# BigBird attention and a Fourier mix on one core: attention values turned into x by VectorE's 32x32 block transposes and 16 small transfers per half pair, and q and k of the last seven pairs turned by VectorE

## The chip, the cores and the metric

The kernel runs on one core of one Trainium2 chip. The time is device time of that core in microseconds (us), as the runs report it; it lies some 2 us above the span of the same run in the trace. The medians of the kernel before range from 1111.3 to 1114.8 us over the five sets of runs, some 0.3%; each experiment is therefore set against runs of the kernel before on the same chip.

## The reference

```python
def _attn_ref(q, k, v, sampled_blocks):            # B, H, S, D = 4, 8, 768, 64; float32
    scores = scale * np.matmul(q, k.transpose(0, 1, 3, 2))
    # mask: blocks of 32; neighbours, first and last block, three sampled blocks per row block
    ...
    scores = np.where(mask, scores, -1000000000.0)
    scores = scores - np.max(scores, axis=-1, keepdims=True)
    attn = np.exp(scores)
    attn = attn / (np.sum(attn, axis=-1, keepdims=True) + 1e-09)
    return np.matmul(attn, v)

def _moe_ref(x, w_ch1, w_ch2):                      # x: (4, 768, 512), the heads side by side
    mixed = np.real(np.fft.fft(np.fft.fft(x, axis=1), axis=2))
    u = x + mixed
    un = (u - mean(u)) / np.sqrt(var(u) + 1e-06)    # over the last axis
    return u + np.maximum(un @ w_ch1, 0.0) @ w_ch2  # 512 -> 2048 -> 512
```

## The kernel before

The kernel walks over 16 pairs of heads, four pairs to a batch. A pair has two halves of queries (384 each), a half has six steps over the keys, and a *slot* is two steps. Each slot issues score products, exponentials (ScalarE), for batches 1 to 3 a mask product (VectorE; in batch 0 the mask is added by a small product on TensorE), and value products into a PSUM bank `o`. Batch 0 also loads and rounds the weights in 32 chunks. From batch 1 on, the Fourier mix and the channel products of the batch before are fed in between the slots. The mixing tail of the last batch closes the run.

A half pair's values come out as head dimension by query and have to be turned into rows of `x`:

```python
def values(u):
    ...
    for i in range(2):
        nc.tensor.matmul(o[D * i:D * i + D, :], vt[:, i, c, :], e[:, i, :],
                         start=(c == 0), stop=(c == C - 1))
    if c == C - 1:
        ...
        oT = sum_p.tile([P, HS], FP32, tag="oT", name="oT")     # one buffer
        nc.scalar.copy(out=oT, in_=o_of.pop((n, half)))
        ...

def place(n, half):
    b, j = pairs[n]
    oT = o_of.pop((n, half))
    if j == 0:
        x_of[b, half] = xp.tile([P, T, DM], FP32, tag=("xA", "xB")[half], name="x")
    xt, at = ps_t.tile([P, 512], FP32, tag="t", name="xt"), bank("t")
    for c in range(T):
        nc.tensor.transpose(xt[:, c * P:(c + 1) * P], oT[:, c * P:(c + 1) * P], ident)
    nc.scalar.copy(out=x_of[b, half][:, :, j * P:(j + 1) * P],
                   in_=xt[:, 0:HS].rearrange("p (c f) -> p c f", c=T))
```

`xp` has two buffers for each half of `x`, so batch 2 writes into the memory of batch 0, whose results must have been stored from there.

The rounding of a weight chunk, in batch 0, is two instructions of ScalarE followed by five of VectorE on the chunk that a transfer of the sync queue brought:

```python
def w_load(i):
    t = room(i % ROOMS, [P, 3 * WN], "wraw", U32)
    nc.sync.dma_start(out=t[:, 0:2 * WN].bitcast(I32), in_=wchunks[i][0])
    ...
def w_round(i):
    ...
    nc.scalar.mul(out=lo.bitcast(FP32), in_=lo, mul=2.0 ** -52)
    nc.scalar.mul(out=a.bitcast(FP32), in_=hi.bitcast(FP32), mul=2.0 ** -112)
    nc.vector.tensor_scalar(out=a, in0=a, ...)             # and four more on VectorE
```

Short jobs (transposes, `place`, mask steps) wait in a list and are put between the products:

```python
while short and (s in (2, 5) or len(short) > 1 or phase == 0 or sl == B * SB):
    short.popleft()[2]()
```

Of the kernel before, what the change touches and what calls it, by code (L numbers as in the profile page):

```python
# [11 lines left out]
FP32 = mybir.dt.float32  # L12
# [6 lines left out]
ACT = mybir.ActivationFunctionType  # L19
# [45 lines left out]
           ((384, 64, 191, 64, 64, -1), (704, -128, 64, 63, 63, -1), (640, 127, 0, 1, 1, 1)))  # L65


def _rows(view, tile):

    got = []  # L70
    for t, p0, runs, jump, n, s0, step in _ORDER:
        if t != tile:
            continue
        at = view[s0:s0 + 1, :]
        row, col = list(at.ap[0])[0], list(at.ap[1])
        if jump > 0:
            got.append((p0, runs * n, bass.AP(tensor=at.tensor, offset=at.offset,
                                              ap=[[jump * row, runs], [step * row, n], col])))
            continue
        for r in range(runs):  # L80
            at = view[s0 + r * jump:s0 + r * jump + 1, :]
            got.append((p0 + r * n, n, bass.AP(tensor=at.tensor, offset=at.offset,
                                               ap=[[step * row, n], col])))
    return got
# [3 lines left out]
def kernel(  # L88
# [14 lines left out]
    nc = tc.nc  # L103

    B, H, S, D = q.shape
    DM = H * D
    FF = w_ch1.shape[1]
    P = 128
    C = S // P
    BLK = 32  # L110
    NB = S // BLK
    NR = sampled_blocks.shape[1]
    HS = S // 2
# [4 lines left out]
    T = C // 2  # L118
# [2 lines left out]
    scale = 1.0 / float(D) ** 0.5  # L121
    KA = D + NB
    NP = H // 2
    LIMIT = 400.0

    const = ctx.enter_context(tc.tile_pool(name="const", bufs=1))

    ident = const.tile([P, P], FP32, name="ident")
# [24 lines left out]
    peaks = const.tile([P, 2 * B * NP], FP32, name="peaks")  # L153

    ld = ctx.enter_context(tc.tile_pool(name="ld", bufs=1))
    ldv = ctx.enter_context(tc.tile_pool(name="ldv", bufs=2))
    tp_p = ctx.enter_context(tc.tile_pool(name="tp_p", bufs=2))
# [19 lines left out]
    def busy(engine, us, after=0.0):  # L177
        when[engine] = max(when[engine], after) + us
        return when[engine]

    def bank(tag):

        at = free[tag].index(min(free[tag]))
        when["PE"] = max(when["PE"], free[tag][at])
        free[tag][at] = float("inf")
        return tag, at

    def give(which, at):
        free[which[0]][which[1]] = at + HOP
# [3 lines left out]
    pairs = [(b, j) for b in range(B) for j in range(NP)]  # L193
    loaded, v_of = {}, {}

    def load_k(n, queue=None):

        b, j = pairs[n]
        kt = loaded.get((n, 1))
        if kt is None:  # L200
            kt = ld.tile([P, C, 2, D], FP32, tag="k", name="kr")
        for i in range(2):
            (queue or nc.sync).dma_start(out=kt[:, :, i, :],
                                         in_=k[b, 2 * j + i].rearrange("(p c) d -> p c d", p=P))
        loaded[n, 1] = kt

    def load_q(n):

        b, j = pairs[n]
        qt = loaded.get((n, 0))  # L210
        if qt is None:
            qt = loaded[n, 0] = ld.tile([P, T, 2, 2, D], FP32, tag="q", name="qr")
        for t in range(T):
            for i in range(2):
                rows = q[b, 2 * j + i][2 * P * t:2 * P * (t + 1), :]
                nc.sync.dma_start(out=qt[:, t, :, i, :],
                                  in_=rows.rearrange("(p r) d -> p r d", r=2))
# [47 lines left out]
    def warm(n):  # L265

        m = ps_m.tile([P, P], FP32, tag="m", name="warm")
        for _ in range(n):
            nc.tensor.matmul(m, ident, ident, start=True, stop=True)
# [158 lines left out]


    turned, e_of, acc_of, o_of, sums_of, x_of, sp_of = {}, {}, {}, {}, {}, {}, {}  # L430
    s_at, e_at, oT_at, acc_at = {}, {}, {}, {}

    def turn(n, a, half):

        t = loaded[n, a]
        if half == 0:
            turned[n, a] = tp_p.tile([P, S], FP32, tag="qk"[a] + "T", name="qk"[a] + "T")
        dst = turned[n, a]
        first = n == 0 and half == 0
        tag, pool = ("m", ps_m) if first and a == 0 else ("t", ps_t)  # L440
        tp, at = pool.tile([P, 512], FP32, tag=tag, name="tp"), bank(tag)
        if a == 0:
            parts = [t[:, c // 2, c % 2, :, :] for c in (range(4, 6) if half else range(4))]
        else:
            parts = [t[:, T * half + c, :, :] for c in range(T)]
        for c, part in enumerate(parts):
            nc.tensor.transpose(tp[:, c * P:(c + 1) * P], part, ident)  # L447
        done = busy("PE", 0.15 * len(parts)) + HOP
        if a == 1:
            nc.scalar.copy(out=dst[:, half * HS:(half + 1) * HS], in_=tp[:, 0:HS])  # L450
            give(at, busy("ACT", 0.5, done))
        else:
            for i, (to, to_jump, frm, jump, cnt, step) in enumerate(_TURNED[half]):
                on, copy = (("DVE", nc.vector.tensor_copy) if n == 0 and (half == 1 or i % 2 == 0)
                            else ("ACT", nc.scalar.copy))
                copy(out=_grid(dst, to, 2, to_jump, cnt, 1),
                     in_=_grid(tp, frm, 2, jump, cnt, step))
                end = busy(on, 0.27 if cnt > 1 else 0.18, done)
            give(at, end)
        if half == 1:  # L460
            flat = t.rearrange("p t r i d -> p (t r i d)" if a == 0 else "p c i d -> p (c i d)")
            nc.scalar.activation(out=flat, in_=flat, func=ACT.Square,
                                 accum_out=peaks[:, 2 * n + a:2 * n + a + 1])
            busy("ACT", 1.05)

    UP = 2 * C
    UNITS = len(pairs) * UP
# [44 lines left out]
    def values(u):  # L512
        n, w = divmod(u, UP)
        half, c = divmod(w, C)
        e = e_of[u]
        busy("PE", 0.75, e_at[u])
        vt = v_of[n]
        if c == 0:
            o_of[n, half] = ps_o.tile([P, HS], FP32, tag="o", name="o")
        o = o_of[n, half]  # L520
# [4 lines that stand above are left out]
            if half == 1:  # L525
                v_of.pop(n)
            oT = sum_p.tile([P, HS], FP32, tag="oT", name="oT")
            nc.scalar.copy(out=oT, in_=o_of.pop((n, half)))
            oT_at[n, half] = busy("ACT", 0.5, when["PE"] + HOP) + HOP
            o_of[n, half] = oT  # L530

    def place(n, half):

        b, j = pairs[n]
        oT = o_of.pop((n, half))
        if j == 0:
            x_of[b, half] = xp.tile([P, T, DM], FP32, tag=("xA", "xB")[half], name="x")
        xt, at = ps_t.tile([P, 512], FP32, tag="t", name="xt"), bank("t")
        for c in range(T):
            nc.tensor.transpose(xt[:, c * P:(c + 1) * P], oT[:, c * P:(c + 1) * P], ident)  # L540
        nc.scalar.copy(out=x_of[b, half][:, :, j * P:(j + 1) * P],
                       in_=xt[:, 0:HS].rearrange("p (c f) -> p c f", c=T))
        give(at, busy("ACT", 0.5, busy("PE", 0.45, oT_at[n, half]) + HOP))

    def into_sums(key, j, sp):
        if j == 0:
# [542 lines left out]
    COVER = 100.0  # L1089
    AHEAD = 2.2  # L1090
    ALONE = 3.0
    LEAVES = 9.0
    SP = UP // SLOT
    SB = SP * NP
    W_PACE = 1.42
# [81 lines left out]
    def slot(sl):  # L1177
# [17 lines left out]
        reuse = n % NP == 0 and phase >= 2  # L1195
        if sl > 0 and s == (5 if reuse else 3) and sl <= B * SB:
            b, j = pairs[n]
            at = oT_at[n, 0]
            if reuse:
                until(lambda: (b - 2, 0) in finished)  # L1200
                at = when["PE"] + LEAVES
            short.append(("t", at, lambda: place(n, 0)))
        if 0 < sl <= B * SB and s == 0 and n % NP != 1:
            short.append(("t", oT_at[n - 1, 1], lambda: place(n - 1, 1)))
        if sl < B * SB and n % NP == 1 and s == 1:
            b = pairs[n - 1][0]
            at = oT_at[n - 1, 1]
            if b >= 2:
                until(lambda: (b - 2, 1) in finished)
                at = when["PE"] + LEAVES  # L1210
            short.append(("t", at, lambda: place(n - 1, 1)))
        if sl > SB and s == 0 and sl <= B * SB:
            short.append(("t", acc_at[n - 1, 1], lambda: total(n - 1)))
        if n + 1 < len(pairs):
            for at, a, half in ((1, 0, 0), (2, 0, 1), (4, 1, 0), (5, 1, 1)):
                if s == at:
                    short.append(("t", 0.0, lambda a=a, half=half: turn(n + 1, a, half)))
            if s == 1:
                load_v(n + 1)
# [15 lines left out]
            channel_step()  # L1235
            gap(max(state["owed"], 0.0))

        while short and (s in (2, 5) or len(short) > 1 or phase == 0 or sl == B * SB):
            short.popleft()[2]()
        if s == 3 and n + 2 < len(pairs):  # L1240
            load_q(n + 2)
        if s == 0 and 0 < n < len(pairs) - 1:
# [26 lines left out]
    state["got"] = 2  # L1269
    turn(0, 1, 0)  # L1270
    turn(0, 0, 0)
    warm(3)
    spread_q(keep_q[0:NB, :], keep)
    w_loads()
    for sl in range(B * SB + 1):
# [112 lines left out]
```

## Time and profile before

In the lines of the profile PE is TensorE's products, PEld its loads of the fixed operand, DVE is VectorE, ACT ScalarE, POOL GpSimd, and SPq the queue of transfers that the sync engine issues. An L with a number is a line of that run's kernel.

| | before |
|---|---|
| time, median of the first 3 runs | 1117.0 us |
| span of the profiled run | 1109.3 us |
| stage 0: to the first mask product of batch 1 | 137.1 us |
| stage 1: to the first store of batch 0's results (batch 1's attention, then mixing) | 298.0 us |
| stage 2: to the first product of the last tail (batches 2 and 3) | 556.1 us |
| tail | 118.1 us |
| TensorE busy | 1067.7 us |

The prediction shows the lines of the page, the stages, the chain and the timelines. Two lines that it does not show: the share of each engine in the chain that ended last, and the granted clock of TensorE in 40 slices (9 is nine tenths of full speed or more).

```profile
PEclk9999999999999999999999999999999999999999
...
PE 85%; DVE 9%; ACT 2%; issue 2%; DMA 0%; POOL 0%; SPq 0%; ACTq 0%; DVEq 0%; POOLq 0%
```

The chain is TensorE's own work for 85% of the span, and the sync queue (SPq) and the transfers have no share of it. No slice of the clock is below 9; its mean is 0.994 (in batch 1, by the prediction's stage table, 0.97).

### The profile page before, as it was taken

How to read it: one execution, taken by the hardware profiler on the slowest of the kernel's cores; microseconds unless marked ns; L12 is line 12 of the kernel's file. 1: busy time of each engine (PE TensorE's matmuls, PEld its weight loads, DVE VectorE, ACT ScalarE, POOL GpSimd, SP SyncE). 2: the span in 40 equal slices, each digit the busy share in tenths (PEclk: the TensorE clock that was granted, in tenths of full speed). 3: DMA queues.
4: the chain of work that ended last, by engine and by line, in shares of the span. 5: the costliest groups of instructions: out<-in, count | busy, mean ns of one | idle time of the engine just before them, and what ended most of it. 6: DMA issues, size and time to landing. Idle time of an engine off the chain costs nothing.

```text
span 1109.3 us, 12468 instructions
## 1 busy us (share of the span) xinstructions
PE 1067.7 (96%) x4446; PEld 544.5 (49%) x4446; DVE 664.8 (60%) x1216; ACT 394.1 (36%) x818; POOL 274.2 (25%) x302
## 2 busy tenths in 40 slices
PE   8999988998899999999999999999999999999996
PEld 3333333544455545444444555454444555568675
DVE  5888878497754525653459355544356446575563
ACT  6788755555212102353443212244330202120210
POOL 1000088688100001245537000344540000000000
PEclk9999999999999999999999999999999999999999
DMA  7756311011000000211110000111000000100001
GB/s 219 208 176 215 93 51 43 15 45 42 1 1 1 0 1 19 66 33 27 43 29 15 1 0 1 51 50 29 1 1 0 1 1 19 39 1 1 1 16 45
DMA packets 65187, 44.30 MB, mean 40 GB/s; under 512 B 52814, under 2 KB 57948, under 8 KB 65116
## 3 DMA queue, kind: packets, MB, share of 16 engines
q1 hardware_dynamic: 63228, 42.62, 13.7%
q10 hardware_dynamic: 1856, 0.79, 0.3%
q8 instruction: 37, 0.61, 0.2%
q14 instruction: 34, 0.28, 0.1%
q0 software_dynamic: 32, 0.01, 0.0%
HBM read 37.11 MB, written 6.29 MB: 39 GB/s over the span
## 4 chain that ended last, share of the span: by engine, by line
PE 85%; DVE 9%; ACT 2%; issue 2%; DMA 0%; POOL 0%; SPq 0%; ACTq 0%; DVEq 0%; POOLq 0%
PE y L954 23%; PE z L898 15%; PE s L478 10%; PE o L522 9%; PE yp L898 7%; PE yy L1017 6%; PE xp L898 4%; DVE e L499 2%; PE tp L447 2%; PE zp L711 1%; PE sp L569 1%; PE zp L682 1%; PE xt L540 1%; PE s L483 1%; PE utp L823 1%
## 5 line engine op out<-in xcount | busy, mean ns | idle before, releaser
L509 POOL TENSOR_TENSOR acc<-acc,e 128x384 f32<-128x384 f32 x192 | 198.3, 1066 | 90.6 <-DVE e L499 90.1
L499 DVE TENSOR_TENSOR e<-s,mask 128x768 f32<-128x768 f32 x144 | 131.2, 951 | 78.4 <-ACT s L497 78.0
L478 PE MATMUL s<-qT,kT 64*128 64x384 f32 x768 | 161.7, 526 | 8.5 <-DVE e L499 7.4
L522 PE MATMUL o<-e,vr 128*64 128x384 f32 x768 | 145.1, 499 | 0.0
L497 ACT ACTIVATE s<-s 128x768 f32<-128x768 f32 x144 | 109.3, 795 | 65.5 <-PE s L478 64.9
L957 DVE TENSOR_TENSOR x<-y,x 128x512 f32<-128x512 f32 x72 | 49.8, 691 | 133.9 <-PE y L954 133.8
L954 PE MATMUL y<-w_sb,hB 128*128 128x512 f32 x288 | 128.4, 595 | 1.1 <-DVE x L957 1.0
L954 PE MATMUL y<-w_sb,hA 128*128 128x512 f32 x288 | 128.8, 594 | 0.6 <-ACT zs L713 0.6
L509 POOL TENSOR_TENSOR acc<-e 128x384 f32<-128x384 f32 x48 | 51.8, 1100 | 231.3 <-DVE e L499 173.2
L903 DVE TENSOR_TENSOR hA<-z,hA 128x384 f32<-128x384 f32 x64 | 35.7, 558 | 111.4 <-PE z L898 111.4
L478 PEld LDWEIGHTS s<-qT,kT 64*128 64x128 f32 x768 | 63.1, 187 | 68.1 <-DVE e L499 25.3
L898 PE MATMUL z<-unT,t 128*128 128x384 f32 x256 | 93.0, 486 | 0.0
L774 POOL TENSOR_SCALAR st<-st 128x1 f32<-128x1 f32 x24 | 6.6, 276 | 344.5 <-DVE st L773 344.1
L954 PEld LDWEIGHTS y<-w_sb,hB 128*128 128x128 f32 x288 | 53.3, 190 | 64.7 <-issue 62.1
L522 PEld LDWEIGHTS o<-e,vr 128*64 128x64 f32 x768 | 46.6, 136 | 73.9 <-issue 71.4
L954 PEld LDWEIGHTS y<-w_sb,hA 128*128 128x128 f32 x288 | 52.9, 190 | 59.6 <-issue 56.6
L907 ACT ACTIVATE hA<-hA 128x384 f32<-128x384 f32 x64 | 33.5, 524 | 123.6 <-DVE hA L903 123.1
L898 PEld LDWEIGHTS z<-unT,t 128*128 128x128 f32 x256 | 48.6, 190 | 33.9
L907 ACT ACTIVATE hB<-hB 128x384 f32<-128x384 f32 x64 | 33.6, 525 | 85.6 <-DVE hB L903 85.6
L898 PE MATMUL z<-t,w_sb 128*128 128x384 f32 x128 | 48.0, 499 | 3.1 <-DVE t L860 3.1
L898 PE MATMUL xp<-unT,w_sb 128*128 128x384 f32 x128 | 47.1, 491 | 1.5 <-ACT zs L713 1.1
L898 PE MATMUL yp<-unT,w_sb 128*128 128x384 f32 x128 | 46.7, 488 | 0.2 <-DVE un L747 0.2
(190 smaller groups left out, 1395.1 us busy)
## 6 DMA issues: line engine op xcount, KB each, us to landing
wraw<-in_moe_w_ch_dram SPq DMA_DIRECT2D x32, 512.0 KB
qr<-in_q_dram SPq DMA_DIRECT2D x90, 64.0 KB
vr<-in_v_dram SPq DMA_DIRECT2D x30, 192.0 KB
kr<-in_k_dram SPq DMA_DIRECT2D x28, 192.0 KB
out_dram<-x SPq DMA_DIRECT2D x16, 128.0 KB
out_dram<-x SPq DMA_DIRECT2D x8, 256.0 KB
out_dram<-x SPq DMA_DIRECT2D x8, 126.0 KB
out_dram<-x SPq DMA_DIRECT2D x4, 252.0 KB
```

The source lines that it names most:

```text
L447: nc.tensor.transpose(tp[:, c * P:(c + 1) * P], part, ident)
L478: nc.tensor.matmul(s[:, i, 0:HS], kT[D * i:D * i + D, c * P:(c + 1) * P], qT[D * i:D * i + D, half * HS:(half + 1) * HS], start=True, stop ...
L497: nc.scalar.activation(out=s[:, :, 0:HS], in_=s[:, :, 0:HS], func=ACT.Exp, scale=scale)
L499: nc.vector.tensor_tensor(out=e, in0=s[:, :, 0:HS], in1=m.broadcast_to([P, 2, HS]), op=ALU.mult)
L509: nc.gpsimd.tensor_add(out=acc, in0=e_of[u - 1][:, i, :] if c == 1 else acc, in1=e[:, i, :])
L522: nc.tensor.matmul(o[D * i:D * i + D, :], vt[:, i, c, :], e[:, i, :], start=(c == 0), stop=(c == C - 1))
L898: nc.tensor.matmul(to, a[:, k, :], c[:, k, :], start=(k == 0), stop=(k == ND // 2 - 1))
L903: tt(out=to, in0=ps, in1=a, op=ALU.add)
L907: nc.scalar.activation(out=h, in_=h, func=ACT.Relu)
L954: nc.tensor.matmul(y, hs[0, half][:, l, m * P:(m + 1) * P], w2_sb[:, 4 * r + l, :], start=(l == 0), stop=(l == 3))
L957: nc.vector.tensor_tensor(out=x[:, m, :], in0=y, in1=x[:, m, :], op=ALU.add)
L1017: nc.tensor.matmul(ps, a[:, k, :], c[k // 2][:, k % 2, :] if isinstance(c, list) else c[:, k, :], start=(k == 0), stop=(k == 3))
```

## The change

Its intent is to take transposes off TensorE, which is 96% busy. (1) The three transposes and two ScalarE copies of each of the 32 half pairs become one VectorE block transpose straight out of PSUM and 16 transfers of 32x3x32 elements (12 KB) on the sync queue, which put the turned blocks where they belong in `x`. (2) For pairs 9 to 15, q and k are loaded as blocks and turned by VectorE. (3) The choice among the short jobs, the first slots and the number of warm-up products change too.

```diff
+    BY_VECTOR = 2 * NP + 1
...
             oT = sum_p.tile([P, HS], FP32, tag="oT", name="oT")
-            nc.scalar.copy(out=oT, in_=o_of.pop((n, half)))
-            oT_at[n, half] = busy("ACT", 0.5, when["PE"] + HOP) + HOP
+            nc.vector.transpose(out=oT, in_=o_of.pop((n, half)))
+            busy("DVE", 0.5, when["PE"] + HOP)
...
     def place(n, half):
-        xt, at = ps_t.tile([P, 512], FP32, tag="t", name="xt"), bank("t")
-        for c in range(T):
-            nc.tensor.transpose(xt[:, c * P:(c + 1) * P], oT[:, c * P:(c + 1) * P], ident)
-        nc.scalar.copy(out=x_of[b, half][:, :, j * P:(j + 1) * P], ...)
+        for g in range(P // BLK):
+            for t in range(P // BLK):
+                nc.sync.dma_start(
+                    out=x_of[b, half][BLK * t:BLK * t + BLK, :, j * P + BLK * g:j * P + BLK * (g + 1)],
+                    in_=oT[BLK * g:BLK * g + BLK, :, t, :])
...
+    def flip_blocks(n, a):
+        ...
+            out = _at(kT, 0, [(1, P), (P, C)])        # k is written strided
+        nc.vector.transpose(out=out, in_=t)
...
-        while short and (s in (2, 5) or len(short) > 1 or phase == 0 or sl == B * SB):
-            short.popleft()[2]()
+        while short and (s in (2, 5) or len(short) > 1 or phase == 0 or r == 0):
+            ready = [i for i in short if max(i[1], min(free[i[0]])) <= when["PE"] + 0.1]
+            if not ready and s not in (2, 5) and r > 0:
+                break
+            item = ready[0] if ready else short[0]
+            ...
-    warm(3)
+    warm(7)
```

Cut: the loads of q and k as blocks, the copies that put q in order, the order of the q transposes in the first slot, a different split of the first copies between VectorE and ScalarE, and a limit (400 to 200) that only the fallback path for large scores uses.

## The prediction

> **What bounds the kernel now.** I began with the first part of the page, then took one table of stages (each engine's busy time in seven stretches), then the chain of work that ended last around a stage boundary, the waits of TensorE, and the timelines of TensorE and of the DMA-issuing queue.
>
> ```profile
> PE 1067.7 (96%) x4446; PEld 544.5 (49%) x4446; DVE 664.8 (60%) x1216; ACT 394.1 (36%) x818; POOL 274.2 (25%) x302
> ```
>
> TensorE is busy in 1067.7 of 1109.3 us, so only 41.6 us of idle time exist and any large gain has to remove TensorE work. The stage table (start:end, length, then busy us of PE, PEld, DVE, ACT, POOL, clock, DMA share, GB/s) says where that holds:
>
> ```profile
> 0.00:138.00 138.00, 129.25 (x794) 48.57 (x794) 109.40 (x258) 104.57 (x213) 3.68 (x14) 1.00 0.61 182
> 138.00:285.00 147.00, 129.85 (x690) 58.29 (x691) 111.81 (x150) 78.89 (x170) 111.93 (x112) 0.97 0.15 38
> 446.00:605.00 159.00, 157.78 (x684) 72.68 (x684) 90.63 (x120) 67.42 (x141) 77.94 (x75) 1.00 0.14 35
> 700.00:840.00 140.00, 137.50 (x583) 63.55 (x582) 68.30 (x102) 54.61 (x107) 58.55 (x60) 1.00 0.08 22
> ```
>
> These are the attention of batch 0, of batch 1, and most of batches 2 and 3 (interleaved with the earlier batches' channel products). In the last two TensorE idles 1.2 and 2.5 us: what is taken from TensorE there is time gained, one for one. In the first two it idles 8.8 and 17.2 us and VectorE is about 79% and 76% busy: here the chain must decide. At the boundary of batch 0 it reads (start, us, what):
>
> ```profile
> 130.59 0.43 DVE wraw L414
> 131.04 0.70 DVE w_sb L416
> 131.77 0.44 DVE wraw L419
> 132.23 0.70 DVE wraw L421
> ...
> 137.16 0.87 DVE e L499
> 138.08 1.78 PE s L478 x8
> ```
>
> So the rounding of the weights on VectorE (five instructions, 2.95 us a chunk, 32 chunks) stands in the queue ahead of the first mask product of batch 1, and TensorE waits for that. VectorE, or what feeds it, sets the end of stage one, although its TensorE looks 94% busy.
>
> The work that goes, and the issue queue, in the two timelines (start, us of the group, engine, line):
>
> ```profile
> 501.55 0.55 PE L540 MATMUL xt<-ident,oT 128*128 128x128 f32 x3
> 501.93 3.60 PE L954 MATMUL y<-w_sb,hA 128*128 128x512 f32 x8
> 505.37 0.60 PE L447 MATMUL tp<-ident,qr 128*128 128x128 f32 x4
> 505.90 1.56 PE L478 MATMUL s<-qT,kT 64*128 64x384 f32 x8
> ...
> 508.83 0.44 PE L447 MATMUL tp<-ident,qr 128*128 128x128 f32 x2
> 509.11 3.60 PE L954 MATMUL y<-w_sb,hA 128*128 128x512 f32 x8
> ```
>
> ```profile
> 174.00 3.82 SPq L216 DMA_DIRECT2D qr<-in_q_dram  x6
> 184.75 1.23 SPq L203 DMA_DIRECT2D kr<-in_k_dram  x2
> 187.85 0.81 SPq L224 DMA_DIRECT2D vr<-in_v_dram  x2
> ```
>
> A group's cost is the distance to the next group's start, since records overlap: three transposes 0.38 us, four 0.53, two 0.28, not the 0.27 us a piece that their medians show. The sync queue needs 3.82/6 = 0.64 us to issue a three-dimensional transfer, and 0.40 for a two-dimensional one, whatever their bytes (64 KB and 192 KB).
>
> [...] This trace has no such transpose; it has a copy of 128x384 out of PSUM, 0.547 us, which I take for oT. [...] the one such transfer in this trace landed in 2.7 us. [...]
>
> **The change, part by part.**
>
> 1. Transposes of values off TensorE. 32 half pairs x 0.38 = 12.2 us, a quarter (3.0) in each batch's stage. 6.1 us of it lie in batches 2 and 3 and count. TensorE idles 7.8 us before these transposes (behind the copies of oT 4.1); a few us of that in batches 0 and 1 can go too.
>
> 2. Transposes of q and k off TensorE for seven pairs. Each pair has 0.53 + 0.28 + 2 x 0.38 = 1.57 us; x7 = 11.0 us, nearly all between 440 and 790 us. It counts. Sum of 1 and 2: 23.2 us of TensorE, of which 17.1 us lie where TensorE is the bound.
>
> 3. VectorE takes 32 transposes of 128x384 at about 0.57 (estimate: copy plus the gap after it) = 18 us, and 14 of 128x768 at about 0.9 (estimate from the mask product of that width, 0.951) = 13 us. In batches 2 and 3 VectorE is 49 to 57% busy, and channel products stand between one slot's products and the next: I allow 2 us of new TensorE waits there. In batch 0 it adds 8 x 0.57 = 4.6 us, less 0.8 for the three qT copies that ScalarE takes over, to the engine that ends the stage. In batch 1 it adds 4.6 us to a VectorE that already makes TensorE wait (scores on mask products, 7.2 us in that stage).
>
> 4. ScalarE loses two copies per half pair, 32 x (0.484 + 0.479) = 30.8 us, 7.7 of it in batch 0, where it is 76% busy and VectorE waits 13.1 us in ten places for its part of the weight rounding. That may give back 2 to 3 us. For seven pairs the q and k copies become six in-order copies and keep their squares; even.
>
> 5. 512 small transfers through the sync queue, 16 per half pair. At 0.64 us each it is 10.2 us of issue per half pair, 20.4 per pair. Beside it, in batch 0, one pair needs 3.8 (q) + 1.2 (k) + 0.8 (v) + about 8.5 weight chunks x 0.37 = 3.1 + about 2.5 of tables = 11.4 us. Sum 31.8 us against a pair's time of about 31 us (six slots of 5.2). The queue is then full in batch 0. There is one oT buffer, so VectorE's next oT transpose waits until the 16 transfers before it are done: 10.2 + about 2.5 us to land = 12.7 us of the 15.5 us of a half pair if the queue comes to them at once, and it often will not. From batch 1 on a pair takes 37 us or more and needs 26: it fits. The engines behind the queue are not the trouble: six q transfers, 1536 pieces of 256 B, took 0.16 of 16 engines for 11.1 us, 28 engine-us; a half pair's 1536 pieces of 128 B should cost no more, 1.8 us over 16 engines.
>
> 6. At a batch's end the scaling of x by the sums must wait for the last 16 transfers (about 12.7 us after the transpose, where it was some 1.5 us on TensorE and ScalarE). VectorE works in order, so the wait also holds mask products or channel sums. Two buffers of PSUM cover some of it: 1 us lost at each of three boundaries. Where x is reused (batches 2 and 3), the transfers wait for the stores of the earlier batch and the next oT transpose for them: about 1 us each.
>
> 7. The changed choice among short jobs (a ready one first, and none if none is ready), the order of the first slots and four more warm-up products: TensorE waits 3.4 us for qT copies before transposes; I count 2 us gained.
>
> Sum: batches 2 and 3 -17.1 + 2 (part 3) = -15; batch 0: -3 to +10, say +3 (VectorE +3.8 and the full queue, less ScalarE's relief and less TensorE work); batch 1: +1 (VectorE +4.6, TensorE -3.0 and fewer waits); boundaries and reuse +5; short jobs -2, waits on oT that vanish outside batch 0: -6 x 1/2 = -3; the choice of 7 warm-ups 0. Together -11 us; since parts 5 and 6 are the most pessimistic terms and the tuning of the slots by its author suggests they were cared for, I take -15 us: 1117 - 15 = 1102 us.
>
> **Rivals.** (a) The sync queue is no bound: issue of an SBUF-to-SBUF transfer costs nearer 0.35 us, or the slack in weight loading absorbs it. For it: small stores and weight loads issue in 0.33 us. Then batch 0 gains 4 us or more and boundaries cost nothing: 1090. (b) The queue or the single oT buffer binds in batch 0 and VectorE stalls: each half pair lengthens by 1 to 2 us, 8 to 16 us, and the gain of batches 2 and 3 is nearly eaten: 1112. For it: the count of part 5. Against it: the queue has idle time now, waiting 28.3 us for rounded weights. (c) VectorE becomes the bound in batches 0 and 1 [...]: +6 to +10, 1108. For it: the chain above; against it, seven pairs only are flipped there, in stages where it is half idle.
>
> **Range and chances.** The stage that is sure gives -15; the rest spreads by about 10 us either way, mostly in batch 0. Range 1088 to 1116. Over 2% faster means under 1094.7, nearly all of the 23.2 us realised or rival (a): 0.28. Within 2%: 0.65. Over 2% slower means over 1139: only if (b) and (c) join: 0.07.
>
> **What would show it.** TensorE busy about 1044 us. The stage from 446 to 840 shorter by about 15 us with TensorE still over 98% busy. StreamTranspose of 128x384 at 0.5 to 0.6 us and of 128x768 at 0.8 to 1.0. Issue of the 16 transfers 0.6 us each; in batch 0 VectorE waiting for their landing before oT transposes. The first score product of batch 1 at 138 to 144 us. I am wrong if TensorE shows long waits behind o or e in batches 2 and 3, if batch 0 ends before 134 us, or if the transfers take well over 0.64 us to issue.

- The trace before has no VectorE transpose. The 0.57 us of part 3 were my estimate from a copy of the same shape (128x384, 0.547 us).
- The transfer that landed in 2.7 us is the only one that GpSimd issues there (13.5 KB). The 2.5 us of landing in part 5, and so the 12.7 us in parts 5 and 6, were my estimate beside that one number.
- That VectorE works in order (part 6) is what the trace before shows at the end of batch 0: ScalarE had `s` ready by 136.15 us, and the mask product began at 137.09 us, behind the rounding (to 136.62 us) and three copies, with no idle time between.

## The result, and the profile after

The kernel after takes **1175.18 us** (median of 4 runs, 1173.98 to 1176.14), the kernel before beside it 1114.76 us (4 runs). All outputs are right. The ratio is **1.0544**, 95% interval 1.0508 to 1.058: slower by over 5%, where the prediction had 1102 us and gave "slower by over 2%" 7 chances in 100. A ratio here is the mean time of one kernel's runs over that of the other's runs of the same rounds, so it is not quite the ratio of the medians that are quoted.

| | before | after | difference |
|---|---|---|---|
| span | 1109.3 | 1174.4 | +65.1 |
| stage 0 | 137.1 | 170.2 | +33.1 |
| stage 1 | 298.0 | 307.1 | +9.1 |
| stage 2 | 556.1 | 579.0 | +22.9 |
| tail | 118.1 | 118.1 | 0.0 |
| TensorE busy | 1067.7 | 1075.5 | +7.8 |

The page of the kernel after, in the same lines as before: busy time of each engine, granted clock, the chain's shares, and (last) the small transfers with their count and size.

```profile
PE 1075.5 (92%) x4274; PEld 534.6 (46%) x4274; DVE 685.6 (58%) x1259; ACT 362.7 (31%) x722; POOL 269.7 (23%) x302
...
PEclk9898899899799999988999999988999999999999
...
PE 66%; SPq 14%; DMA 9%; DVE 6%; issue 2%; ACT 2%; DVEq 0%; POOL 0%; ACTq 0%
...
x<-oT SPq DMA_DIRECT2D x512, 12.0 KB
```

Three things stand there. TensorE runs 172 products fewer (4274 for 4446) and yet is busy 7.8 us longer. Its clock is reduced in nine of the 40 slices (mean 0.963 for 0.994). And 23% of the chain now belongs to the sync queue and to transfers, which had none. The stage table says where (start:end, length, then busy us of PE, PEld, DVE, ACT, POOL, clock, DMA share, GB/s); of before I show the long stage, of after the first and the long one.

```profile
442.50:994.80 552.30, 546.18 (x2059) 272.06 (x2057) 298.03 (x513) 171.72 (x354) 153.22 (x164) 1.00 0.08 20
```

```profile
0.00:170.00 170.00, 139.54 (x774) 51.17 (x778) 111.28 (x259) 98.40 (x200) 3.68 (x14) 0.91 0.51 151
...
484.50:1059.90 575.40, 544.37 (x1937) 261.75 (x1935) 309.25 (x540) 153.86 (x292) 148.94 (x164) 0.98 0.12 25
```

In the first stage no engine is full: TensorE idles 30.5 of 170 us, VectorE 58.7. In the long stage TensorE idled 6.1 us before and idles 31.0 us after. What ends these waits is in the tables of waits. First TensorE's (waiting line, what it waited for, us in total, times, the longest):

```profile
PE o L585 <- DVE oT L591: 43.2, 13, 6.9
PE s L541 <- ACT e L557: 10.3, 3, 6.2
```

Before, the value products had no idle time in front of them (the last number of their line on the page):

```profile
L522 PE MATMUL o<-e,vr 128*64 128x384 f32 x768 | 145.1, 499 | 0.0
```

Then, after the change, ScalarE's and the sync queue's:

```profile
ACT wraw L446 <- DMA wraw<-in_moe_w_ch_dram: 29.5, 8, 11.4
...
SPq L604 <- DMA out_dram<-x: 24.1, 5, 11.3
```

TensorE waits 43.2 us to start value products, because the one bank `o` is still held: the VectorE transpose has not read it. 24.9 of those 43.2 us fall in four places of stage 2, 12.7 in five places of stage 0, 5.6 in stage 1. ScalarE waits 29.5 us for the transfers of weight chunks, which it did not do before; the exponentials that stand behind these in its order come late, and in stage 0 TensorE's scores wait 10.3 us for them (the longest wait: ScalarE idle 8.02 us until a chunk at 96.63 us, the exponentials at 99.25 us, TensorE idle 6.20 us until 100.11 us). The queue waits 24.1 us for stores out of `x`.

**Batch 0.** The timeline of the sync queue (start, us of the group, what, count) and the pieces of the chain between 34 and 171 us:

```profile
59.94 12.93 SPq L604 DMA_DIRECT2D x<-oT  x16
72.97 1.01 SPq L260 DMA_DIRECT2D vr<-in_v_dram  x2
74.09 0.83 SPq L437 DMA_DIRECT2D wraw<-in_moe_w_ch_dram  x2
75.02 1.18 SPq L368 DMA_DIRECT2D tab<-in_cos_s_dram  x2
76.29 12.33 SPq L604 DMA_DIRECT2D x<-oT  x16
```

```profile
55.79 7.60 DMA wraw<-in_moe_w_ch_dram
...
71.50 1.37 SPq L604
74.56 7.04 DMA wraw<-in_moe_w_ch_dram
```

The groups touch: from 34.6 to about 160 us the queue is hardly ever free (the longest gap between two groups is 3.2 us, at 154.5 us). A set of 16 transfers takes 10.4 to 13.2 us, and the two weight chunks of 74.09 stand behind such a set, so the chain runs from a chunk (55.79) through the set (71.50) to the next chunk (74.56). In this stretch 32% of the chain is weight transfers and 24% is the issue of the small ones. That is part 5's full queue, but as the bound of the stage and not as a small addition.

**The reuse of x.** At 488 us, in pair 8, `x` of batch 0 has just been stored. The sync queue, VectorE and TensorE in that place (the bracket is idle time before the group, and what ended it):

```profile
488.14 10.31 SPq L604 DMA_DIRECT2D x<-oT  x16
```

```profile
500.05 0.58 DVE L591 STREAM_TRANSPOSE oT<-o 128x384 f32<-128x384 f32 x1 [6.84 <-DMA x<-oT]
```

```profile
490.62 1.51 PE L585 MATMUL o<-e,vr 128*64 128x384 f32 x8
...
500.69 2.83 PE L585 MATMUL o<-e,vr 128*64 128x384 f32 x8 [6.28 <-DVE oT L591]
```

The 16 transfers could not be issued before the last store had landed at 487.94 us. They need 10.31 us of issue, the last lands 1.8 us after its issue began, and until then the only `oT` buffer is not free. The next transpose waits for it, the bank `o` waits for the transpose, and TensorE idles 6.28 us. Then eight value products take 2.83 us where the same eight took 1.51 us ten microseconds earlier: the clock has fallen. The granted clock is 0.50 from 500 to 506 us, where it was 1.00 from 488 to 494 us, and the products take 1.9 times as long. This fits TensorE being busy longer with less work. There are four such places, two halves of pairs 8 and 12.

The length of a wait alone did not decide it. Eight value products took 2.83 us in e4 after a wait of 2.14 us (at 52.86 us, shown below), and 1.51 us in the kernel after behind one of 2.93 us (at 74.86 us; granted clock 1.00 from 74 to 78 us).

**The instructions themselves.** By tile: duration in ns as min/median/max.

```profile
L604 SPq DMA_DIRECT2D x<-oT x512: 585/597/1806, 34.6 to 912.6; - x171
L591 DVE STREAM_TRANSPOSE oT<-o x32: 562/576/583, 34.0 to 901.5; 128x384 f32<-128x384 f32 x32
```

```profile
L517 DVE STREAM_TRANSPOSE kT<-kb x7: 1489/1506/1535, 310.5 to 852.2; 128x768 f32<-128x768 f32 x7
```

The transpose out of PSUM (predicted 0.57 us) and the issue (predicted 0.64) are what was expected; q's transpose, 0.969 us, too (0.9). Only k's, which is written strided, is off: 1.506 us.

### The profile page after: what moved, and what is told of

The parts are those of the page before. It is cut to its first block, busy times and chain, and to the rows that moved or that the text cites. A ratio compares the mean times of both kernels' runs of the same rounds, so it can differ in the third digit from the quotient of the medians.

```text
span 1174.4 us, 12689 instructions
## 1 busy us (share of the span) xinstructions
PE 1075.5 (92%) x4274; PEld 534.6 (46%) x4274; DVE 685.6 (58%) x1259; ACT 362.7 (31%) x722; POOL 269.7 (23%) x302
## 4 chain that ended last, share of the span: by engine, by line
PE 66%; SPq 14%; DMA 9%; DVE 6%; issue 2%; ACT 2%; DVEq 0%; POOL 0%; ACTq 0%
PE y L1017 19%; PE z L961 13%; SPq L604 11%; PE yp L961 7%; PE s L541 6%; PE o L585 6%; PE yy L1080 6%; DMA wraw<-in_moe_w_ch_dram 4%; PE xp L961 3%; DMA out_dram<-x 2%; DVE e L562 1%; PE zp L774 1%; DMA x<-oT 1%; SPq L252 1%; PE zp L745 1%
## 5 line engine op out<-in xcount | busy, mean ns | idle before, releaser
L585 PE MATMUL o<-e,vr 128*64 128x384 f32 x768 | 156.6, 532 | 43.2 <-DVE oT L591 43.2
L541 PE MATMUL s<-qT,kT 64*128 64x384 f32 x768 | 169.0, 544 | 23.3 <-ACT e L557 10.3
L572 POOL TENSOR_TENSOR acc<-e 128x384 f32<-128x384 f32 x48 | 47.3, 1007 | 259.8 <-DVE e L562 203.2
L585 PEld LDWEIGHTS o<-e,vr 128*64 128x64 f32 x768 | 49.0, 143 | 126.6 <-issue 71.2
```

Of the source, the lines that this page charges most:

```text
L541: nc.tensor.matmul(s[:, i, 0:HS], kT[D * i:D * i + D, c * P:(c + 1) * P], qT[D * i:D * i + D, half * HS:(half + 1) * HS], start=True, stop ...
L572: nc.gpsimd.tensor_add(out=acc, in0=e_of[u - 1][:, i, :] if c == 1 else acc, in1=e[:, i, :])
```

## The experiments

My theory after reading the traces was: in batch 0 the sync queue's issue time is the bound (it delays the weights); in batches 2 and 3 the single `oT` buffer turns the issue into TensorE's idle time at the four places of reuse. The first rival was that the single buffer does it in batch 0 too, because the next transpose waits for the 16 transfers before it. The second was that VectorE itself, with its new work, is what is late. Where the expectations use letters, Q stands for the queue, B for the buffer, V for VectorE's new work, S for the changed schedule and L for the bank of `o`. Thirteen kernels ran. They are told by question, and all are read by the stages of the table above:

| run | time (n) | ratio to before, 95% | stage 0 | stage 1 | stage 2 |
|---|---|---|---|---|---|
| before | 1114.76 (4) | | 137.1 | 298.0 | 556.1 |
| after | 1175.18 (4) | 1.0544, 1.0508 to 1.058 | 170.2 | 307.1 | 579.0 |
| e1_flips_only | 1109.37 (4) | 0.9978, 0.9948 to 1.0007 | 141.9 | 294.7 | 552.3 |
| e2_values_only | 1176.41 (2) | 1.0579, 1.0546 to 1.0611 | 168.3 | 304.0 | 583.3 |
| e3_two_oT | 1153.07 (2) | 1.0369, 1.0335 to 1.0403 | 168.8 | 306.3 | 559.7 |
| e4_pool_b0 | 1165.73 (2) | 1.0483, 1.0438 to 1.0527 | 152.7 | 313.7 | 576.1 |
| e5_schedule_only | 1113.61 (4) | 1.002, 1.0003 to 1.0037 | 140.6 | 296.7 | 556.2 |
| e6_flips_oldstart | 1110.57 (4) | 0.9994, 0.9978 to 1.0011 | 140.3 | 298.0 | 552.2 |
| e7_small_where_room | 1112.71 (2) | 1.0013, 0.9993 to 1.0033 | 140.6 | 306.0 | 546.2 |
| e8_flips11_oldstart | 1120.98 (4) | 1.0095, 1.0076 to 1.0114 | 140.5 | 308.6 | 552.3 |
| e9_pool_and_two | 1145.19 (2) | 1.0297, 1.0252 to 1.0342 | 152.9 | 314.1 | 560.5 |
| e10_late_only | 1103.07 (4) | 0.9918, 0.9885 to 0.995 | 140.6 | 296.6 | 547.5 |
| e11_late_oldstart | 1100.89 (6) | 0.9898, 0.9873 to 0.9923 | 137.0 | 296.7 | 546.2 |
| e12_late_noflip | 1106.62 (4) | 0.9956, 0.9915 to 0.9996 | 137.1 | 298.4 | 550.3 |
| e13_pool_copy | 1153.49 (2) | 1.038, 1.034 to 1.042 | 140.0 | 313.3 | 578.6 |

### Which half of the change costs the time: e1 and e2

e1 places the values as before (TensorE and ScalarE) and keeps the rest of the change; the switch below is used again later with other conditions. e2 keeps the transfers and turns no q and k by VectorE.

```diff
+    def BY_PE(n, half):
+        return True
...
-            nc.vector.transpose(out=oT, in_=o_of.pop((n, half)))
+            if BY_PE(n, half):
+                nc.scalar.copy(out=oT, in_=o_of.pop((n, half)))
+            else:
+                nc.vector.transpose(out=oT, in_=o_of.pop((n, half)))
...  # place: the three transposes and the copy of before where BY_PE holds
```

> Only the flips of q and k stay: the values go back through TensorE and ScalarE as in the kernel before, so no small transfers. Theory Q (the 16 issues a half pair fill the sync queue in batch 0 and hold the reuse of x later) and theory B (the single oT buffer makes VectorE wait for its 16 transfers): the loss is all in the values part, the first mask product comes at 138 us or before instead of 170, and the total is about 1115 - 11 = 1104 us. Theory V (the added VectorE work, above all the 1.5 us transpose of k, costs more than TensorE gains): 1115 us or more.

```diff
-    BY_VECTOR = 2 * NP + 1
+    BY_VECTOR = len(pairs)
```

> Only the values part stays, all pairs' q and k are turned on TensorE. Q and B: the flips were a gain of about 11 us, so 1175 + 11 = 1186 us. V: the flips were a loss, so 1165 us or less. First mask product stays at about 170 us in each.

e1 takes 1109.37 us, e2 1176.41 us. The whole loss belongs to the values' half of the change (the transposes of `o` on VectorE together with the transfers), and the turned q and k lose nothing (e1 with the changed schedule is level with before). Both totals miss what was expected (1104 us for e1; 1186, or 1165 at most, for e2), because what the turned q and k gain is small: stage 2 of e2 is 4.3 us longer than that of the kernel after (583.3 and 579.0).

### Queue or buffer: e3, e4, e9

e3 gives every second half pair of batch 0 and of pairs 4, 8 and 12 another buffer, taken from a pool that is unused then. e4 leaves the buffer single and lets GpSimd, nearly idle in batch 0 (3.68 us), issue that batch's transfers. e9 does both.

```diff
-            oT = sum_p.tile([P, HS], FP32, tag="oT", name="oT")
+            if half == 1 and (n < NP or n % NP == 0):
+                oT = zc_p.tile([P, 2, KS], FP32, tag="zc", name="oT2").rearrange(
+                    "p a b -> p (a b)")[:, 0:HS]
+            else:
+                oT = sum_p.tile([P, HS], FP32, tag="oT", name="oT")
```

> A second oT buffer for odd half pairs of batch 0 and for the pairs that reuse x; transfers and queue unchanged. B: batch 0 recovers (first mask product at 138 to 145 us) and the 25 us of waits of values products on oT at the reuse of x go: about 1120 us. Q: the queue still needs over 32 us for a pair in batch 0, first mask product at 160 us or later; only the reuse waits and the slow clock after them go (some 30 us): about 1145 us.

```diff
-                nc.sync.dma_start(
+                (nc.gpsimd if n < NP else nc.sync).dma_start(
```

> In batch 0 the 16 transfers are issued by GpSimd, which is idle there; one oT buffer as in the changed kernel. Q: the sync queue is free for weights and q, k, v, ScalarE no longer waits for weights (29.5 us of waits gone), first mask product at 138 to 146 us, total about 1145 us; the reuse waits in batches 2 and 3 stay. B: the chain transpose, 16 transfers, next transpose is as long as before or longer, so first mask product stays at 165 us or later and the total at about 1175 us.

e9 is both edits together.

> Both remedies of the third and fourth experiment: GpSimd issues batch 0's transfers, and odd half pairs of batch 0 and of the pairs that reuse x have an oT buffer of their own. Q with a rest for B: with the queue out of the way the single buffer is the next limit in batch 0, so its first mask product comes at 141 to 145 us (152.7 with the queue alone, 168.8 with the buffer alone), and the total is about 1153 - 26 = 1127 us. If something else (VectorE's extra transposes, GpSimd's issue) holds batch 0, it stays at 150 us or later and the total at 1135 or more.

The two stages come apart cleanly. In stage 0 a second buffer does nothing (168.8 for 170.2 us), and it does nothing on top of the other issuer either (e9 152.9, e4 152.7), while the other issuer gives back 17.5 us (152.7). GpSimd needs 0.545 us to issue such a transfer (median of 128), the sync queue 0.597. So in batch 0 the queue is the cause and the buffer is not. In stage 2 it is the other way round: the second buffer gives back 19.3 us (559.7 for 579.0) and the issuer of batch 0 only 2.9. The rival is refuted for batch 0 and holds in part for the places where `x` is reused: e3's stage 2 is still 13.5 us longer than that of e7 below, which has no transfers there (546.2), and two of the four waits, 9.9 us together, are left in it. The transfer engines themselves are not what is full in batch 0: their busy share is 0.51 there after the change and was 0.61 before. e4 moves the issue and the queue together, so it does not separate the time of issue from the order within the queue.

152.7 us is still 15.6 us more than before, with the queue relieved, and later than the 138 to 146 us expected of it; of e9's two cases the second came (150 us or later). In e4 the value products of batch 0 wait 11.0 us in four places for the transpose. VectorE's timeline at one of them, and TensorE's there:

```profile
51.62 0.69 DVE L458 TENSOR_TENSOR w_sb<-w_sb,wraw 128x512 f32<-128x512 f32 x1
52.23 0.57 DVE L591 STREAM_TRANSPOSE oT<-o 128x384 f32<-128x384 f32 x1
```

```profile
52.86 2.83 PE L585 MATMUL o<-e,vr 128*64 128x384 f32 x8 [2.14 <-DVE oT L591]
```

The transpose comes right behind the last of the five instructions of a weight chunk (L450 to L458), which VectorE works off one after the other from 49.25 us without idle time, although TensorE had done the bank's last products by 47.44 us. Before, ScalarE emptied the bank (0.484 us a copy) and the value products waited 0.0 us. This gave a new theory.

### Is it the bank behind VectorE's queue: e13

e13 is e4 with a ScalarE copy of `o` out of PSUM in batch 0, which VectorE then turns from SBUF. VectorE's work is the same; only the bank is freed by another engine.

```diff
+            src = o_of.pop((n, half))
+            if n < NP:
+                oc = zc_p.tile([P, 2, KS], FP32, tag="zc", name="oc").rearrange(
+                    "p a b -> p (a b)")[:, 0:HS]
+                nc.scalar.copy(out=oc, in_=src)
+                src = oc
-            nc.vector.transpose(out=oT, in_=o_of.pop((n, half)))
+            nc.vector.transpose(out=oT, in_=src)
```

> As the fourth experiment (GpSimd issues batch 0's transfers), but in batch 0 ScalarE copies the sums of values out of PSUM first, and VectorE transposes the copy; one oT buffer. Theory L (the rest in batch 0 is the bank of o, held until VectorE's in-order queue gets past a chunk of weight rounding): the four waits of 11 us on oT before values products go, with the slow clock after them, and the first mask product comes at 140 to 145 us instead of 152.7, total about 1155 us. Rival (VectorE is simply too full with eight more transposes): the weight rounding ends as late as before, first mask product at 150 us or later, though the waits of TensorE on oT go.

Stage 0 falls from 152.7 to 140.0 us, where the rival of this run, that VectorE is simply too full, expected 150 us or later. TensorE's waits in it hold no line of `o` any more; the two longest that are left are one wait each, for the first mask product of batch 1 and for the copies of q in the first slot:

```profile
PE s L541 <- DVE e L562: 5.2, 1, 5.2
PE s L541 <- DVE qT L492: 4.0, 1, 4.0
```

So the 33.1 us of stage 0 divide into 17.5 (queue, e4), 12.7 (bank behind VectorE, e13) and 2.9 that are left, of which the next section tells. The division holds for this order: no run frees the bank while the sync queue still issues batch 0's transfers. The total of e13 is 1153.49 us all the same. Batch 0 repaired in this way costs time in stage 1: 313.3 us for 307.1, as in e4 and e9 (313.7, 314.1). What fits is that GpSimd, which sums e from batch 1 on, is still issuing the last transfers of batch 0 (15 of them from 143.83 to 151.87 us). In stage 1 of e13 these issues hold 4.8% of the chain, and VectorE waits 6.9 us for the sums (`e` behind `acc`), a wait that the kernel after does not have there. No run removed this one cost alone.

### The changed schedule: e5 and e6

e5 is the changed schedule without either half of the change (BY_PE true and BY_VECTOR at the number of pairs). e6 is e1 with the first slots, the copies' split and the three warm-up products of before.

```diff
-    BY_VECTOR = 2 * NP + 1
+    BY_VECTOR = len(pairs)        # on top of e1
```

> Neither values nor flips: only the changed first slots (second half of the first q turned two slots later and copied by VectorE behind weight rounding, first copies on ScalarE alone, 7 warm-up products) and the changed choice among short jobs. Theory S: they cost what the flips gained in the first experiment, by a 4 us wait of the first scores on the qT copy and the slow clock after it: first mask product at about 142 us, total 1112 + 6 = 1118 us. Rival: the schedule is neutral, 1112 us, and the flips are worth only 3 us by themselves.

```diff
-                on, copy = (("DVE", nc.vector.tensor_copy) if n == 0 and half == 1
+                on, copy = (("DVE", nc.vector.tensor_copy) if n == 0 and (half == 1 or i % 2 == 0)
-            for at, a, half in ((1, 0, 0), (2 if n > 0 else 3, 0, 1), (4, 1, 0), (5, 1, 1)):
+            for at, a, half in ((1, 0, 0), (2, 0, 1), (4, 1, 0), (5, 1, 1)):
-    warm(7)
+    warm(3)
```

> Flips alone as in the first experiment, with the first slots of the kernel before (the changed choice among short jobs stays). S: the wait of 4 us on the qT copy and the slow stretch go, first mask product at 135 to 138 us, total about 1103 us, 0.8% under the kernel before. Rival (schedule neutral): 1109 us as in the first experiment.

The schedule costs 3.5 us in stage 0 (140.6 for 137.1), and as a whole 0.2%, where I had counted 2 us gained. The wait and the slow clock that theory S names are in the trace of the kernel after: its scores wait 4.04 us for the copies of q until 27.86 us, and the granted clock is 0.58 from 28 to 32 us. The old first slots alone do not bring it back (140.3). e11, further down, has the old first slots and, in batch 0, also the old choice among short jobs, and is at 137.0. So the old choice in batch 0 is needed. Whether it would do alone is open; no run has it without the old first slots.

### Where the transfers fit: e7, e10 and e8

e7 uses the transfers wherever I thought that there is room: not in batch 0 and not in pairs 8 and 12. e10 leaves out batch 1 as well. e8 puts the values on TensorE everywhere and turns q and k from pair 5 on, in batch 1 too, to see what VectorE bears there.

```diff
+        return n < NP or n in (8, 12)             # e7, in BY_PE
+        return n < 2 * NP + 1 or n == 3 * NP      # e10, in BY_PE
```

> The change with the values placed through TensorE in batch 0 and for the two pairs that reuse x (pairs 8 and 12), by transfers elsewhere (20 of 32 half pairs). Q: no full queue in batch 0, no waits on oT at the reuse of x; first mask product at 142 us (the late start stays), total 1105 to 1112 us. Rival (each set of 16 transfers costs by itself, by landing, VectorE order or the clock): about 5/8 of the loss stays, 1130 us or more.

> The change with transfers for the values of six pairs only (9 to 11 and 13 to 15), TensorE placing the others; flips and schedule as changed. From the stages of earlier runs: batch 0 as in the flips-only run 141.9, batch 1 and the channel products 294.7, batches 2 and 3 as in the seventh run 546.2, end 118.1: span 1101, time about 1103 us. If the stages don't add up (batch 2 inherits a delay), 1109 us as flips only.

```diff
-    BY_VECTOR = 2 * NP + 1
+    BY_VECTOR = NP + 1            # e8, on top of e6
```

> As the sixth, but with q and k of eleven pairs turned by VectorE (pairs 5 to 15 instead of 9 to 15). If TensorE bounds batch 1 too: another 4 x 1.6 = 6 us gained, about 1097 us. If VectorE does (it makes TensorE wait 7 us there): 4 x 2.5 us more on it, nothing gained or up to 6 us lost, 1103 to 1109 us.

Compare e7 with e1, which differ only in who places the values of pairs 4 to 7, 9 to 11 and 13 to 15. In stage 2 e7 gains 6.1 us (546.2 for 552.3), in stage 1 it loses 11.3 (306.0 for 294.7). The queue in batch 1 of e7:

```profile
156.82 10.41 SPq L626 DMA_DIRECT2D x<-oT  x16
167.34 3.87 SPq L252 DMA_DIRECT2D qr<-in_q_dram  x6
...
172.65 10.78 SPq L626 DMA_DIRECT2D x<-oT  x16
```

and, of TensorE's waits in its stage 1, the one that e1 does not have at all:

```profile
PE o L594 <- DVE oT L604: 6.0, 3, 4.7
```

Two sets start 15.8 us apart, with 3.87 and 1.24 us of loads between them. So the queue is nearly full again. Over the eight sets of batch 1 (the last starts at 259.91 us) a set follows the other after 14.7 us on average, so a pair takes 29 to 32 us, not the 37 us from which I had worked. The stage is long because the mixing comes after its four pairs, not because its pairs are slow. Beside the wait for `o`, the wait of the transposes for normalised rows (`utp` behind VectorE's `un`) is 8.3 us for 3.1 in e1. These two differences, 6.0 and 5.2, come to 11.2 of the 11.3 us.

e8 shows the same tightness from the other side. Four more pairs of q and k on VectorE, 2.5 us each, cost 10.6 us in stage 1 (308.6 for 298.0 in e6):

```profile
PE s L550 <- DVE e L571: 17.1, 8, 4.2
```

TensorE waits 17.1 us for mask products there (9.0 in e6) and 11.1 us for normalised rows (3.1). The total, 1120.98 us, is worse than both expectations. VectorE had no room for this in batch 1.

Without transfers at the reuse, stage 2 is 546.2 (e7) or 547.5 us (e10) for 579.0, so these places, two half pairs each in pairs 8 and 12, cost 32.8 us: 24.2 us of TensorE idle time (31.0 for 6.8) and 8.6 us of longer busy time, which goes with the lowered clock (0.98 for 1.00).

### A version that beats both: e11, and its half e12

e11 is e10 with the first slots of before and, in batch 0, the old choice among short jobs. e12 is e11 without the turned q and k.

```diff
-            if not ready and s not in (2, 5) and r > 0:
+            if not ready and s not in (2, 5) and r > 0 and phase > 0:
                 break
-            item = ready[0] if ready else short[0]
+            item = ready[0] if ready and phase > 0 else short[0]   # with e6's and e10's edits
```

> As the tenth, with the first slots of the kernel before and, in batch 0, its choice among short jobs. Batch 0 back to 137.1: about 1098 us, 1.2% under the kernel before. If the schedule's cost in batch 0 is made up later (as in the sixth run, where the old first slots brought nothing), 1103 us.

```diff
-    BY_VECTOR = 2 * NP + 1
+    BY_VECTOR = len(pairs)        # e12, on top of e11
```

> As the eleventh, without flips: all q and k turned on TensorE. If the flips are worth 11 us where TensorE is the bound, as predicted: 11 us slower than the eleventh, about 1109. If about 4 us, as the stage of batches 2 and 3 showed (556.2 against 552.3): about 1102 us.

e11 takes 1100.89 us (1099.73 to 1101.57, 6 runs), 1111.39 for the kernel before beside it: a ratio of 0.9898 with an interval that excludes 1. It is the fastest kernel. 1.0% is less than the 2% from which a run counts as faster, and it is what the best version that I ran is worth.

```profile
PE 1057.0 (96%) x4326; PEld 532.2 (48%) x4326; DVE 675.8 (62%) x1242; ACT 379.2 (35%) x759; POOL 270.5 (25%) x302
```

TensorE is busy 10.7 us less than before and the span is 11.2 us shorter (1098.1): once nothing waits for transfers, what is taken off TensorE is time gained, as the prediction said of these stages. By stages it is 0.1, 1.3 and 9.9 us. Against e12 (1106.62; stage 2 550.3) the turned q and k are worth 4.1 us in stage 2.

That is less than the 1.57 us a pair of part 2. I added up the distance from each group of products to the next in stage 2 of e12 and of e11. In e12 75 transposes of q and k, some 25 groups, take 11.07 us. In e11 they are gone, but value products grow by 1.68 us, scores by 1.43, the transposes of normalised rows by 1.43, channel products by 1.37, and others by 1.1: 7.0 us together. So a group that takes 0.44 us until the next one starts saves about 0.16 us when it is removed. Part of the difference is waiting: TensorE's busy time in stage 2 falls by 6.2 us (545.8 to 539.6), and its idle time grows by 2.1 (4.5 to 6.6), 1.7 of it one wait for a mask product of VectorE. So a group saves some 0.25 us of busy time. Why whatever adjoins it takes over the rest is not shown by these runs. For values the same count came out better: e7 against e1 has 4.8 us of transposes less and gains 6.1 us in stage 2, of which 4.1 are busy time and 2.1 idle time that went.

## Why the prediction was wrong

**What held.** The bound of the long stage was read rightly: TensorE work removed there is time, and with the waits out of the way (e11) 9.9 us came. The durations of the transpose (0.576 for 0.57) and of the issue (0.597 for 0.64) held, so rival (a) is out. Of rival (c), k's transpose did take longer than the 0.9 us of part 3 (1.506 us), but VectorE idles 58.7 of the 170 us of stage 0, so it does not bound that stage as a whole. Rival (b) named the queue in batch 0 and had the mechanism; it had 8 to 16 us for it. Its single buffer is not what binds there (e3).

**The step that failed first: part 5's weighing.** The working was right: "31.8 us against a pair's time of about 31 us". A full queue was then entered as "say +3" for batch 0. A queue that needs as long as the stage has no slack, so each weight chunk in it arrives late by whatever stands ahead of it (a set of 16 transfers took 10.4 to 13.2 us), and VectorE's rounding, which the chain already showed as the end of stage 0, starts late. The term measured 17.5 us (e4). Its second sentence, "From batch 1 on a pair takes 37 us or more and needs 26: it fits", divided the 147 us of its second stretch by four, although the four pairs do not fill it; pairs take 29 to 32 us (e7), and instead of "+1" stage 1 cost 11.3 us (e7 against e1), of which the wait for `o` is 6.0.

**A step that was missing: who frees the bank.** Part 3 counted VectorE's load, 4.6 us in batch 0, and part 4 counted ScalarE's relief. Neither asked whose queue the reading of `o` stands in. It moved from an engine that was prompt (value products waited 0.0 us) to one that has 2.95 us of rounding ahead of it, with one bank: 12.7 us (e13).

**Part 6's "about 1 us each".** The steps were named, that the transfers wait for stores and the next transpose for the transfers. The size was not worked out, although the numbers were there: 10.2 us of issue and the landing (1.8 us, as measured at 497.85 us), with the next half pair's values due after a few products. A place measured 32.8/4 = 8.2 us. Of that about 6 us is idle and about 2 us the clock after it, which no part of the sum had. Of the part's other term, a batch's end, VectorE's waits for the last transfers before it scales `x` came to 7.0 us in two places; how much of that reached TensorE was not taken apart.

**Part 2.** "A group's cost is the distance to the next group's start" is right as a reading and wrong as a saving: 4.1 us in stage 2 in place of 11.0.

**Part 7.** "2 us gained" was 3.5 us lost in stage 0 (e5).

**The choice at the end.** The sum was -11, and I took -15, with the words that "parts 5 and 6 are the most pessimistic terms". They were the most optimistic: the sum with the measured terms is 33.1 (stage 0), 9.1 (stage 1) and 32.8 - 9.9 = 22.9 (stage 2), together the 65.1 us by which the span grew. That the author's tuning would have cared for it was no evidence from the profile. Of the signs that I had named for being wrong, "long waits behind o or e in batches 2 and 3" is the one that came.

## What to carry to other kernels

Here small transfers were paid in issue time of one queue (0.597 us each, 10.31 us for 16, and 1.8 us for the last to land). Count such time per stretch against what the queue already carries, and when the sum comes near the stretch (31.8 of about 31 us), treat every load behind it as late rather than adding the excess: it was 17.5 us and not 3. When an operation moves to another engine, ask which buffer it frees and what stands before it in the new engine's queue, above all where there is one PSUM bank (12.7 us here). Apply such a change only where the bound is the engine that it relieves: here three pairs in each of the last two batches gave 1% (with the turned q and k), and all sixteen cost 5%.
